# One more PSUM bank for attention while a chunk's down groups are queued, and two output tiles loaded ahead of output weights

## The chip, the cores and the metric

The kernel runs on one core of a Trainium2 chip. The core has five engines that run side by side, each with its own queue of instructions in program order: TensorE (PE in the profile; its weight loads are PEld) multiplies matrices, VectorE (DVE) and ScalarE (ACT) work element by element and are the two that empty PSUM, GpSimd (POOL) works on SBUF alone, and SyncE (SP) issues the transfers between memory and SBUF. They wait for each other through semaphores. PSUM has eight banks, each 128 partitions by 512 float32 numbers; a matmul writes into one of them, and the bank can be given to the next tile only after its last reader is done. The metric is the device time of the whole kernel in microseconds (us).

## What is computed

The reference, cut to what matters (S = 2048 tokens, D = 576, H = 32 heads of 18, F = 4608, four segments of L = 512 tokens):

```
g = sigmoid((x * gate_w).sum(-1))
# a: attention inside each segment, plus a memory of the segments before
for s in range(4):
    p = softmax(q_s @ k_s.T * scale + mask)          # causal in the segment
    o_s = sig(beta) * (phi(q_s) @ M) / (phi(q_s) @ z) + (1 - sig(beta)) * (p @ v_s)
    M += phi(k_s).T @ v_s ;  z += phi(k_s).sum()
a = concat(o_s) @ wo
# b: a gated feed-forward
b = (silu(x @ w_gate) * (x @ w_up)) @ w_down
out = g * a + (1 - g) * b
```

Every float32 operand that matters is split into a high and a low part, so that one product is three matmuls (high by high, high by low, low by high).

## The kernel before

**Three phases.** The first makes q, k, v and the memory term and writes them to DRAM scratch. The second, four fifths of the program, does two things at once: the feed-forward, and attention inside the segments. The third transposes attention's output tiles, multiplies them with the output weights, mixes with the gate and stores.

**The feed-forward sets the pace.** The hidden dimension is cut into 36 pieces f of 128; the tokens are taken in two halves (`half`). For each (half, f), the loop at L1007, seven products (`seven`, L993; Strassen's seven in place of eight) make gate and up for two blocks of 512 tokens. One `seven` is six matmuls at L998 and one at L1001, 512 columns each. They use PSUM banks 0, 1 and 2. ScalarE and VectorE combine them (L1058 to L1083), and the product of silu(gate) and up is split into `hh` and `hl` (ScalarE's copy, then VectorE's difference: L128 and L129, L940 and L941).

Three f make a chunk (`CH`, q = f % 3 is the place in it). When a chunk is complete, sixteen **down groups** are queued in `groups` (`feed`, L959): eight token tiles by two column halves. One group (`down_group`, L841) is nine matmuls (L851) into a bank, and then VectorE adds the bank into `ya` (L856; a plain copy, L854, in the first chunk).

**Ticks.** After each of the seven products, and once more between the sixth and the seventh, `tick` (L1034) is called: eight ticks k = 0 to 7 per f. A tick first issues the transfers of the down weights and then calls `beat` (L943). A beat first runs whatever was put off to it: `defer(n, fn)` puts fn n beats later, and functions of one beat run in the order in which they were put there. Then it interleaves down groups and attention. In the f after a chunk (q = 0), `SHARE` (L48) lets no group run in ticks 0 and 1, two in each of ticks 2 and 3, and three in each of the others; so the sixteen groups wait through ticks 0 and 1 and run from tick 2 on. Attention advances by one step at each such beat, by two in the beats with three groups; in f without groups it advances only in some of the ticks 0 to 4.

**Attention** is a generator (`att_gen`, L792). It works on pairs of heads; a pair of one segment is a unit of five score banks and one value product, so six steps. A step does, in this order: turn exponentials of earlier steps into float16 (`p_bank`, VectorE L752 and GpSimd L753); exponentials of the score bank of the step before (`e_bank`, ScalarE L738, which is the bank's last reader); matmuls of a new score bank (`s_bank`, TensorE L720) and its row minimum (VectorE L726). At every sixth step, in place of a score bank, the value product of the unit before (`v_unit`, TensorE L768 and L769, emptied by VectorE at L775). So a score bank taken at one step becomes free only after ScalarE's exponentials of the next step.

**Who gets which bank.** The bank of a tile is chosen while the program is written, by name, and is fixed from then on. `ts_tile` (L119) serves scores and value products: the least recently taken of banks 5, 6, 7, 3 and 4 when no group is queued, and of 5 and 6 alone as soon as `groups` holds anything, thus also in ticks 0 and 1. `group_tile` (L122) serves down groups: the least recently taken of 3, 4 and 7. `oldest` (L114) picks and notes the order.

**Where the second phase ends.** When attention has no step left, `c_open` (L864) runs once, in the beat of (second half, f = 34, tick 1). It gives attention's SBUF space to the third phase and defers, in beats: six loads of output weights (`wo_load`, L883, transfer L888, high part L891, low part L892) at beats 1, 2, 4, 5, 8 and 9; the first output tile at beat 2; the gate at 3 and 4; the second output tile at beat 6. `c_load` (L894) issues two transfers for a tile, attention's output (`o`, L897) and the memory term (`me`, L901). `c_tr` (L911) adds them on GpSimd (L913, L914), transposes on TensorE (L917, L919) and splits. A weight load needs one of four buffers named `raw`, which the last feed-forward weights still hold. SyncE issues in program order, so a transfer that waits for its buffer holds up those behind it. After the loop the third phase goes through sixteen tiles; with the first of them run the last sixteen down groups.

Of the kernel before, what the change touches and what calls it, by code (L numbers as in the profile page):

```python
# [12 lines left out]
F32 = mybir.dt.float32  # L13
# [28 lines left out]
HALF = ((2, 3), (0, 1))  # L42
TICK = ((0.57, 1.0), (0.47, 1.0))
QUIET = (5, 6, 7)
LEAD = 3
HIGH = (2, 3, 3, 7, 7, 8, 9)
LOW = (5, 6, 7, 8, 9, 10, 11)
# [18 lines left out]
def gated_mix(ctx, tc, xT, xrest, wf, wfr, wfh, wd, wv, wo, beta, cmask, ident, bmask, out):  # L66
# [3 lines left out]
    def pool(st, name, bufs, side="left", space=None):  # L70
        if space is None:
            return st.enter_context(tc.tile_pool(name=name, bufs=bufs, side=side))
        return st.enter_context(tc.tile_pool(name=name, bufs=bufs, space=space))
# [12 lines left out]
    ps = pool(ctx, "ps", 1, space=bass.MemoryType.PSUM)  # L86
# [12 lines left out]
    def banks(*ids):  # L99
        turn = cycle(ids)  # L100
        return lambda shape=(P, L): ps.tile(list(shape), F32, name=f"bank{next(turn)}")
# [8 lines left out]
    x_tile = banks(1)  # L110
    y_tile = banks(2)
    taken = {}

    def oldest(*ids):  # L114
        n = min(ids, key=lambda i: taken.get(i, 0))
        taken[n] = len(taken) + max(taken.values(), default=0) + 1
        return n

    def ts_tile(shape=(P, L)):  # L119
        return ps.tile(list(shape), F32, name=f"bank{oldest(5, 6) if groups else oldest(5, 6, 7, 3, 4)}")  # L120

    def group_tile(shape=(P, L)):  # L122
        return ps.tile(list(shape), F32, name=f"bank{oldest(3, 4, 7)}")

    groups = []

# [121 lines left out]
    def w_make(half, f, LOW=LOW):  # L248
# [5 lines left out]
        def total(j, p, q, sub=True):  # L254
            src[j] = rp.tile([P, 2, P], F32, name="ws", bufs=3)
            (nc.gpsimd.tensor_sub if sub else nc.gpsimd.tensor_add)(src[j], p(), q())  # L256
# [8 lines left out]
        def keep(j):  # L265
            nc.sync.dma_start(wc[f, j], f32(ops[j]).rearrange("p a k n -> p (a k n)"))

        todo = [(LEAD - 2, lambda: total(1, lambda: a21, lambda: a22, False)),
                (LEAD - 1, lambda: total(2, lambda: src[1], lambda: a11)),
                (LEAD + 2, lambda: total(4, lambda: a11, lambda: a21)),  # L270
                (LEAD + 4, lambda: total(5, lambda: a12, lambda: src[2]))]
        for j in range(7):
            todo += [(HIGH[j], lambda j=j: high(j)), (LOW[j], lambda j=j: low(j))]
            if half == 0 and f < KEPT:
                todo.append((LEAD + j + 3, lambda j=j: keep(j)))
        return sorted(todo, key=lambda t: t[0])
# [407 lines left out]
    with ExitStack() as st:  # L684
# [3 lines left out]
        def defer(k, fn):  # L688
            while len(due) < k:
                due.append([])  # L690
            due[k - 1].append(fn)
# [21 lines left out]
        def s_bank(z):  # L713
            u, n = divmod(z, 5)
            qs, ks = qst[u % NST], kst[u % NST]
            m = mbs[u % 2]
            t = ts_tile()
            for c, pr, i in SPLAN[n]:
                w = P * (i + 1)
                nc.tensor.matmul(t[:, c:c + w], qs[:KR, pr, P * i:P * i + P], ks[:KR, pr, 0:w],  # L720
                                 start=True, stop=True)
            for c, pr, i in SPLAN[n]:
                w = P * (i + 1)
                k = pr * 4 + i
                scr = kp.tile([P, L], BF, name="scr", bufs=1)
                nc.vector.tensor_tensor_reduce(scr[:, :w], t[:, c:c + w], cm[:, L - w:L], -SCALE, 3.0e38,  # L726
                                               OP.add, OP.min, m[:, k:k + 1])
            cur["t", z] = t
# [30 lines left out]
        def v_unit(u):  # L759
            g, hf = divmod(u, 2)  # L760
            s, b = divmod(u, 16)
            t = ts_tile([P, 2, 4, 3 * E])
            todo = [(5 * u + n, pr, i, j, c // P + j) for n in range(5) for c, pr, i in SPLAN[n] for j in range(i + 1)]
            for n, (z, pr, i, j, c) in enumerate(todo):
                h = 2 * b + pr
                v = VP[4 * s + h // 8][:, j, h % 8].rearrange("p t e -> p (t e)")
                pt = cur["x", z]
                nc.tensor.matmul(t[:, pr, i, :], pt[:, c], v, start=(n == 0), stop=False, skip_group_check=True)  # L768
                nc.tensor.matmul(t[:, pr, i, 0:2 * E], pt[:, 4 + c], v[:, 0:2 * E], start=False,  # L769
                                 stop=(n == len(todo) - 1), skip_group_check=True)  # L770
            for n in range(5):
                cur.pop(("x", 5 * u + n))
            if hf == 0:
                accs[g] = ap.tile([P, 2, 8, E], F32, name="acc")
            nc.vector.tensor_reduce(accs[g][:, hf], t.rearrange("p a i (t e) -> p (a i) e t", t=3),  # L775
                                    axis=AX.X, op=OP.add)
# [64 lines left out]
        def down_group(c, i, hf, hs, ws, ya, half):  # L841
            b, k = divmod(i, 4)
            cs = (slice(0, 320), slice(320, D))[hf]
            t = (pair_tile if cps else group_tile)([P, 320])[:, :cs.stop - cs.start]
            n = 0
            for f in range(CH * c, CH * c + CH):
                hh, hl = (z[:, b, P * k:P * k + P] for z in hs[half, f])
                d = ws[half, f]
                dh, dl = d[:, 0], d[:, 1]
                for p, q in ((hh, dh), (hh, dl), (hl, dh)):  # L850
                    nc.tensor.matmul(t, p, q[:, cs], start=(n == 0), stop=(n == 3 * CH - 1))  # L851
                    n += 1
            if c == 0:
                nc.vector.tensor_copy(ya[:, i, cs], t)  # L854
            else:
                nc.vector.tensor_add(ya[:, i, cs], t, ya[:, i, cs])  # L856
            if c == FT // CH - 1 and hf and half == 0:
                stores.append((ffd[i], ya[:, i]))


        wos, tiles = [], {}
        order = [4 * s + k for s in HALF[0] + HALF[1] for k in range(4)]

        def c_open():  # L864
            if cps:
                return
            ast.close()
            cps.append(pool(st, "cp", 2, side="right"))
            for hf in range(2):
                wos.append(cps[0].tile([P, 2, NT, 288], F32R, name=f"wo{hf}", bufs=1))  # L870
            for n, (hf, z) in zip((1, 2, 4, 5, 8, 9), ((0, 0), (0, 1), (0, 2), (1, 0), (1, 1), (1, 2))):
                wo_load(n, hf, slice(96 * z, 96 * z + 96))
            defer(2, lambda: tiles.update({0: c_load(0)}))
            defer(3, lambda: nc.scalar.activation(gg, gg, AF.Exp, scale=-1.0))
            defer(4, gates)
            defer(6, lambda: tiles.update({1: c_load(1)}))

        def gates():
            nc.vector.tensor_scalar_add(gg, gg, 1.0)
# [3 lines left out]
        def wo_load(n, hf, c):  # L883
            box = []

            def load():
                box.append(raw_tile()[:, :96 * NT].rearrange("p (k n) -> p k n", n=96))
                nc.sync.dma_start(box[0], wo[:, :, 288 * hf + c.start:288 * hf + c.stop])  # L888

            defer(n, load)  # L890
            defer(n + 5, lambda: nc.scalar.activation(wos[hf][:, 0, :, c], box[0], AF.Copy))  # L891
            defer(n + 7, lambda: nc.vector.tensor_sub(wos[hf][:, 1, :, c], box[0], f32(wos[hf][:, 0, :, c])))  # L892

        def c_load(n):  # L894
            tt = order[n]
            o = cps[0].tile([P, 640], F32, name="o", bufs=3)
            nc.sync.dma_start(o[:, 0:D], atd[tt])  # L897
            me = None
            if tt >= 4:
                me = cps[0].tile([P, D], F32, name="me", bufs=3)  # L900
                nc.sync.dma_start(me, med[tt])  # L901
            return o, me
# [40 lines left out]
        def beat(k=None, half=0):  # L943
            for fn in due.popleft() if due else ():
                fn()
            busy = 1 if groups else 0
            share = 2 if k is None else SHARE[k]
            for n in range(max(share, 1)):
                if groups and n < share:
                    down_group(*groups.pop(0))  # L950
                if n % 2 or (not busy and (n or k in QUIET)):
                    continue
                credit[0] += 0.5 if k is None else TICK[half][busy]
                if credit[0] >= 1:
                    credit[0] -= 1
                    if next(att, att) is att:
                        c_open()
# [143 lines left out]
        while next(att, att) is not att:  # L1101
            pass
        c_open()
        while due:
            for fn in due.popleft():
# [90 lines left out]
```

## Time and profile before

| what | value |
|---|---|
| median of 3 runs | 1739.13 us |
| lowest, highest | 1737.43, 1739.77 us |
| the profiled execution | 1738.29 us |
| its span, first to last instruction | 1736.6 us |
| mean granted TensorE clock | 0.998 |
| VectorE, ScalarE, GpSimd busy | 1370.0, 1094.1, 935.1 us |
| transfers | 328.05 MB, mean 189 GB/s |

How to read the rows that follow. In a timeline: start in us from the first instruction, duration in us, engine, line of the program, operation, what is written from what, shape, how many alike in a row; in square brackets the idle time of the engine before it and the operation that ended it. In a list of waits: who waited for whom, total us, times, longest. Matmuls run in a pipeline: the end of one is modelled, and the next may start before it. A group's name as L851 is a line of the kernel printed above.

### The profile page before, as it was taken

How to read it: one execution, taken by the hardware profiler on the slowest of the kernel's cores; microseconds unless marked ns; L12 is line 12 of the kernel's file. 1: busy time of each engine (PE TensorE's matmuls, PEld its weight loads, DVE VectorE, ACT ScalarE, POOL GpSimd, SP SyncE). 2: the span in 40 equal slices, each digit the busy share in tenths (PEclk: the TensorE clock that was granted, in tenths of full speed). 3: DMA queues.
4: the chain of work that ended last, by engine and by line, in shares of the span. 5: the costliest groups of instructions: out<-in, count | busy, mean ns of one | idle time of the engine just before them, and what ended most of it. 6: DMA issues, size and time to landing. Idle time of an engine off the chain costs nothing.

```text
span 1736.6 us, 34910 instructions
## 1 busy us (share of the span) xinstructions
PE 1714.6 (99%) x11868; PEld 1482.5 (85%) x11868; DVE 1370.0 (79%) x3231; ACT 1094.1 (63%) x2198; POOL 935.1 (54%) x1194
## 2 busy tenths in 40 slices
PE   9999999999999999999999999999999999999999
PEld 7899978888888888887887788888888888888899
DVE  6557588988899889887989677787888777887655
ACT  7766585776677567666755755665766576566511
POOL 4434645666666656565666455555555555555121
PEclk9999999999999999999999999999999999999999
DMA  8654499999998889997879976776778677766544
GB/s 281 237 185 155 149 306 191 222 215 203 202 232 197 176 205 207 190 190 193 205 149 266 265 173 142 180 178 162 152 180 182 139 155 180 169 135 166 157 148 137
DMA packets 524002, 328.05 MB, mean 189 GB/s; under 512 B 411184, under 2 KB 460336, under 8 KB 523824
## 3 DMA queue, kind: packets, MB, share of 16 engines
q1 hardware_dynamic: 523824, 325.83, 76.6%
q8 instruction: 93, 1.52, 0.4%
q14 instruction: 85, 0.70, 0.1%
HBM read 165.76 MB, written 76.09 MB: 139 GB/s over the span
## 4 chain that ended last, share of the span: by engine, by line
PE 81%; ACT 9%; DVE 4%; DMA 2%; issue 2%; POOL 1%; SPq 1%; DVEq 0%; ACTq 0%; POOLq 0%
PE bank L998 30%; PE bank L851 26%; PE bank L151 10%; PE bank L1001 5%; PE bank L720 4%; PE bank L768 2%; ACT L1075 1%; PE bank L769 1%; ACT L991 1%; ACT pe L738 1%; PE bank L406 1%; PE bank L452 1%; ACT row L1075 1%; PE bank L342 1%; DVE hl L941 1%
## 5 line engine op out<-in xcount | busy, mean ns | idle before, releaser
L753 POOL TENSOR_TENSOR p<-pe,p 128x512 f16<-128x512 f32 x320 | 374.9, 1171 | 454.1 <-DVE p L752 437.4
L851 PE MATMUL bank<-dw,hh 128*128 128x320 f32 (+1 forms) x2304 | 489.9, 305 | 2.7 <-ACT hh L128 1.4
L851 PEld LDWEIGHTS bank<-dw,hh 128*128 128x128 f32 x2304 | 382.6, 190 | 14.0 <-DVE ya L856 1.6
L738 ACT ACTIVATE pe<-bank,mb 128x512 f32<-128x512 f32 (+3 forms) x512 | 246.4, 523 | 218.8 <-DVE mb L726 213.4
L851 PE MATMUL bank<-dw,hl 128*128 128x320 f32 (+1 forms) x1152 | 341.1, 296 | 0.2 <-DVE hl L129 0.2
L726 DVE CUSTOM_DVE_ANT_0 scr<-bank,cm 128x512 bf16<-128x512 f32 (+3 forms) x512 | 246.3, 481 | 7.9 <-PE bank L720 1.2
L851 PEld LDWEIGHTS bank<-dw,hl 128*128 128x128 f32 x1152 | 218.6, 190 | 0.4 <-DVE hl L129 0.4
L856 DVE TENSOR_TENSOR ya<-bank,ya 128x320 f32<-128x320 f32 x352 | 157.7, 453 | 72.3 <-PE bank L851 71.6
L1001 PE MATMUL bank<-xr,rh 128*128 128x512 f32 x504 | 196.5, 390 | 0.0
L746 POOL TENSOR_SCALAR_AFFINE_SELECT pe<-pe 128x256 f32<-128x256 f32 (+1 forms) x320 | 151.1, 473 | 31.3 <-ACT pe L738 20.2
L752 DVE CAST p<-pe 128x512 f16<-128x512 f32 x320 | 147.5, 461 | 0.0
L256 POOL TENSOR_TENSOR ws<-raw 128x256 f32<-128x256 f32 x140 | 123.6, 883 | 18.3 <-DMA raw<-in_wf_dram 7.2
L720 PE MATMUL bank<-kst,qst 108*128 108x512 bf16 (+3 forms) x512 | 125.4, 306 | 4.7 <-ACT pe L738 4.7
L1001 PEld LDWEIGHTS bank<-xr,rh 128*128 128x128 f32 x504 | 94.7, 188 | 20.5
L941 DVE TENSOR_TENSOR hl<-row,hh 128x512 fp32r<-128x512 f32 x120 | 101.6, 847 | 10.9 <-ACT hh L940 10.6
L1068 ACT ACTIVATE row<-bank 128x512 f32<-128x512 f32 x72 | 43.1, 599 | 94.6 <-PE bank L1001 94.5
L1075 ACT ACT_TABLE_LOAD x72 | 92.4, 1283 | 1.3
L1073 DVE TENSOR_TENSOR row<-bank,row 128x512 f32<-128x512 f32 x72 | 49.7, 690 | 55.0 <-ACT bank L1072 54.9
L991 ACT ACT_TABLE_LOAD x72 | 92.4, 1283 | 1.0
L151 PE MATMUL bank<-xo,qhi 128*128 128x512 f32 x264 | 83.1, 396 | 0.1
L1072 ACT ACTIVATE bank<-bank 128x512 f32<-128x512 f32 x72 | 42.0, 584 | 65.0 <-PE bank L1001 64.6
L256 POOL TENSOR_TENSOR ws<-raw,ws 128x256 f32<-128x256 f32 x70 | 56.6, 808 | 48.4 <-DVE wo__22573 L263 10.9
(2166 smaller groups left out, 4119.1 us busy)
## 6 DMA issues: line engine op xcount, KB each, us to landing
raw<-in_wf_dram SPq DMA_DIRECT2D x140, 256.0 KB
rh<-rc SPq DMA_DIRECT2D x72, 336.0 KB
dc<-dw SPq DMA_DIRECT2D x36, 576.0 KB
dw<-dc SPq DMA_DIRECT2D x36, 576.0 KB
stk<-q SPq DMA_DIRECT2D x32, 384.0 KB
draw<-in_wd_dram SPq DMA_DIRECT2D x36, 288.0 KB
rc<-rt SPq DMA_DIRECT2D x42, 224.0 KB
vd<-vps SPq DMA_DIRECT2D x8, 912.0 KB
```

The lines of the kernel that those rows point to most:

```text
L151: nc.tensor.matmul(t, st[n], mv[n], start=(n == 0), stop=(n == 13))
L256: (nc.gpsimd.tensor_sub if sub else nc.gpsimd.tensor_add)(src[j], p(), q())
L720: nc.tensor.matmul(t[:, c:c + w], qs[:KR, pr, P * i:P * i + P], ks[:KR, pr, 0:w], start=True, stop=True)
L726: nc.vector.tensor_tensor_reduce(scr[:, :w], t[:, c:c + w], cm[:, L - w:L], -SCALE, 3.0e38, OP.add, OP.min, m[:, k:k + 1])
L738: nc.scalar.activation(pe[:, c:c + w], t[:, c:c + w], AF.Exp, bias=m[:, k:k + 1], scale=SCALE)
L746: nc.gpsimd.affine_select(d, d, pattern=pat, compare_op=OP.is_ge, fill=0.0, base=0, channel_multiplier=1)
L752: nc.vector.tensor_copy(p[:, 0], pe)
L753: nc.gpsimd.tensor_sub(p[:, 1], pe, p[:, 0])
L851: nc.tensor.matmul(t, p, q[:, cs], start=(n == 0), stop=(n == 3 * CH - 1))
L856: nc.vector.tensor_add(ya[:, i, cs], t, ya[:, i, cs])
L998: nc.tensor.matmul(t, w[:, p, z], x[z][:, q], start=first and n == 0, stop=False, skip_group_check=True)
L1001: nc.tensor.matmul(t, rem[:, RPOS[j]], XR[j], start=False, stop=True, skip_group_check=True)
```

## The change

Two things are changed. First, the choice of banks. While all sixteen groups of a chunk are still queued (so in ticks 0 and 1 of the f after a chunk), scores and value products choose among banks 5, 6 and 7 in place of 5 and 6. The order of taking is replaced by a clock that goes up by one at each bank taken by attention or a group and at each beat; a bank that attention takes is noted as taken `HELD` = 4 units later than the clock, a group's bank 1 unit later, and the lowest note is picked. Second, in `c_open`, the loads of the first two output tiles are deferred ahead of the output weights: the first stays at beat 2 but comes before the weight load of that beat, the second moves from beat 6 to beat 3.

```diff
+HELD = 4
...
     taken = {}
-
-    def oldest(*ids):
+    clock = [0]
+
+    def soonest(ids, held):
         n = min(ids, key=lambda i: taken.get(i, 0))
-        taken[n] = len(taken) + max(taken.values(), default=0) + 1
+        clock[0] += 1
+        taken[n] = clock[0] + held
         return n
 
     def ts_tile(shape=(P, L)):
-        return ps.tile(list(shape), F32, name=f"bank{oldest(5, 6) if groups else oldest(5, 6, 7, 3, 4)}")
+        ids = (5, 6, 7, 3, 4) if not groups else (5, 6, 7) if len(groups) == 16 else (5, 6)
+        return ps.tile(list(shape), F32, name=f"bank{soonest(ids, HELD)}")
 
     def group_tile(shape=(P, L)):
-        return ps.tile(list(shape), F32, name=f"bank{oldest(3, 4, 7)}")
+        return ps.tile(list(shape), F32, name=f"bank{soonest((3, 4, 7), 1)}")
...
                 wos.append(cps[0].tile([P, 2, NT, 288], F32R, name=f"wo{hf}", bufs=1))
+            defer(2, lambda: tiles.update({0: c_load(0)}))
+            defer(3, lambda: tiles.update({1: c_load(1)}))
             for n, (hf, z) in zip((1, 2, 4, 5, 8, 9), ((0, 0), (0, 1), (0, 2), (1, 0), (1, 1), (1, 2))):
                 wo_load(n, hf, slice(96 * z, 96 * z + 96))
-            defer(2, lambda: tiles.update({0: c_load(0)}))
             defer(3, lambda: nc.scalar.activation(gg, gg, AF.Exp, scale=-1.0))
             defer(4, gates)
-            defer(6, lambda: tiles.update({1: c_load(1)}))
...
             for fn in due.popleft() if due else ():
                 fn()
             busy = 1 if groups else 0
+            clock[0] += 1
```

## The prediction

> **What bounds the kernel.** I read the page first, then TensorE's own waits, then the timeline around each wait.
>
> ```profile
> span 1736.6 us, 34910 instructions
> PE 1714.6 (99%) x11868; PEld 1482.5 (85%) x11868; DVE 1370.0 (79%) x3231; ACT 1094.1 (63%) x2198; POOL 935.1 (54%) x1194
> ```
>
> TensorE (PE) is busy for 1714.6 of 1736.6 us; no other engine comes near. Whatever the change wins must come out of the 22 us in which it stands idle, or out of gaps that the busy time hides. The next view says for whom it stood: line, who released it, total us, times, longest.
>
> ```profile
> PE bank L720 <- ACT pe L738: 4.7, 6, 1.2
> PE bank L768 <- ACT pe L738: 3.1, 2, 1.9
> ...
> PE bank L917 <- POOL o L913: 1.1, 1, 1.1
> ```
>
> L720 is a score matmul, L768 the first matmul of a value product, and L738 the exponentials that empty a score bank. So eight times, 7.8 us in all, attention found no free bank. L917 is the transpose of an output tile and waited once for L913, which adds its two loaded halves. These three rows are what the change can reach. One stall in full, on TensorE:
>
> ```profile
> 624.85 0.39 PE L1001 MATMUL bank<-xr,rh 128*128 128x512 f32 x1
> 626.39 0.38 PE L720 MATMUL bank<-kst,qst 108*128 108x512 bf16 x1 [1.16 <-ACT pe L738]
> ...
> 628.01 0.39 PE L1001 MATMUL bank<-xr,rh 128*128 128x512 f32 x1
> 628.24 0.46 PE L851 MATMUL bank<-dw,hh 128*128 128x320 f32 x2
> ...
> 632.49 0.30 PE L851 MATMUL bank<-dw,hh 128*128 128x320 f32 x1
> ```
>
> Without a wait the next matmul starts 0.23 us after L1001 (628.24 - 628.01). Here it starts 1.54 us after: 1.31 us is lost, 0.16 more than the 1.16 that is printed as idle. Counting L1001 matmuls puts this stall at tick 1 of f = 21: the sixteen down groups of a chunk have been queued, none has run, and the score tile may take bank 5 or 6 only. All eight stalls lie at tick 1 of such an f (two were value products, in the same place). L851 at 628.24 is the chunk's first down group.
>
> [...]
>
> **The change, part by part.** *Third bank.* I wrote out which bank each tile takes under both rules. The order of instructions on every engine stays what it was (outside the two output tiles), and so do all durations; only the waits on banks move. In each of the 22 chunks whose groups start at tick 2, one of the two score or value tiles of ticks 0 and 1 now takes bank 7. In all eight stalled places the tile then finds a bank that was emptied over 4 us earlier, going by the times of before. Removed: 7.8 + 8 x 0.16 = **9.1 us**. Two more score matmuls lose under 0.3 us together; I count them at nothing.
>
> *What comes in its place.* Bank 7 is then missing for the first groups. Before, the third group (tick 3) took a bank that attention had left long ago. Now, in the 14 chunks where bank 7 went out at tick 1, the first groups have banks 3 and 4 alone, so the third takes the first one's bank and must wait for VectorE's add (L856, L854 in the first chunk) of the first group. The rows: the add, then the third group's first matmul.
>
> ```profile
> 390.00 0.30 PE L851 MATMUL bank<-dw,hh 128*128 128x320 f32 x1
> 390.28 0.48 DVE L856 TENSOR_TENSOR ya<-bank,ya 128x320 f32<-128x320 f32 x1
> ...
> 1477.83 0.48 DVE L856 TENSOR_TENSOR ya<-bank,ya 128x320 f32<-128x320 f32 x1
> 1478.14 0.30 PE L851 MATMUL bank<-dw,hh 128*128 128x320 f32 x1
> ```
>
> At 390 the add ends at 390.76 (0.76 after the matmul started); with 0.05 us for the signal, the lag at which the eight stalls ended, TensorE would wait 0.81 us. At 1478 it ends at 1478.31: 0.21. In the other twelve the add ends 0.15 to 1.7 us before the matmul of before, so nothing is due there unless TensorE comes earlier, and in the stalled chunks it does. Is VectorE able to come earlier too? In the chunk of the stall above:
>
> ```profile
> 625.65 0.69 DVE L129 TENSOR_TENSOR hl<-row,hh 128x512 fp32r<-128x512 f32 x1 [1.22 <-ACT hh L128]
> ...
> 630.68 1.22 DVE L941 TENSOR_TENSOR hl<-row,hh 128x512 fp32r<-128x512 f32 x1
> 631.82 0.48 DVE L856 TENSOR_TENSOR ya<-bank,ya 128x320 f32<-128x320 f32 x1
> ```
>
> These are the first and the last two of eleven rows; only the first prints an idle time. From 625.65, where ScalarE releases it, to the add's end at 632.30 VectorE runs without a gap; it is behind, not waiting for TensorE. So the add stays where it is. The third group started at 632.49; 1.31 us earlier is 631.18, and it would wait until 632.35: 1.17 of the 1.31 us is given back. The same subtraction, first and last stalled chunk (the stall, the add, the third group):
>
> ```profile
> 262.80 0.22 PE L720 MATMUL bank<-kst,qst 108*128 108x128 bf16 x1 [0.93 <-ACT pe L738]
> 267.52 0.48 DVE L854 COPY ya<-bank 128x320 f32<-128x320 f32 x1
> 268.87 0.30 PE L851 MATMUL bank<-dw,hh 128*128 128x320 f32 x1
> ...
> 1591.80 0.19 PE L768 MATMUL bank<-v,pt 128*128 128x57 bf16 x1 [1.22 <-ACT pe L738]
> 1596.90 0.48 DVE L856 TENSOR_TENSOR ya<-bank,ya 128x320 f32<-128x320 f32 x1
> 1598.54 0.30 PE L851 MATMUL bank<-dw,hh 128*128 128x320 f32 x1
> ```
>
> First: won 0.93 + 0.16 = 1.09, add over at 268.00, so 268.05 - (268.87 - 1.09) = 0.27 back. Last: won 1.38, add over at 1597.38, 0.27 back. The six between these two, by the same working: 1.17 (above), 0.33 in one, 0.2 in one (up to 0.4; there VectorE has a gap and can follow in part), nothing in three. Returned in the eight: 2.2. New waits in all: 0.81 + 0.21 + 2.2 = **3.3 us**; from below 1.0, if every add follows TensorE; from above 9.1 + 1.0, if the eight give everything back.
>
> *Held longer.* A score bank counts as taken 4 units later than a group's 1. At a chunk's end the first free score tile so prefers a group's bank. By the times of before, the closest such pick leaves 0.9 us and the others more: nothing.
>
> *Two output tiles.* Tile 0's loads go ahead of the second output-weight load, tile 1's ahead of the third. SyncE's queue runs in order:
>
> ```profile
> 1622.69 6.78 SPq L888 DMA_DIRECT2D raw<-in_wo_dram  x2
> ...
> 1635.98 1.46 SPq L888 DMA_DIRECT2D raw<-in_wo_dram  x2
> 1637.49 0.62 SPq L897 DMA_DIRECT2D o<-atd  x1
> ...
> 1645.78 0.66 PE L917 MATMUL bank<-idt,o 128*128 128x128 f32 x4 [1.09 <-POOL o L913]
> ...
> 1649.21 0.65 DVE L892 TENSOR_TENSOR wo<-raw,wo 128x480 fp32r<-128x480 f32 x1
> ...
> 1650.00 0.32 PE L151 MATMUL bank<-wo,oh 128*128 128x288 f32 x1
> ```
>
> The weight loads (L888) wait for buffers, and tile 1 (1637.49) stood behind the pair at 1635.98. In the new order it goes out at about 1630, 7 us earlier, and L917's wait of 1.09 + 0.16 = 1.25 us goes. No weight load is held up, since those wait for buffers longer than two issues take. What is late next: the last low part of the output weights (L892) ends at 1649.86, and the matmul that reads it starts at 1650.00. Only 0.14 us is won unless that weight arrives earlier, which two tile loads out of its way may give by 0.2 us. I take **0.4 us**; between nothing and 1.25.
>
> **The sum.** 9.1 - 3.3 + 0.4 = 6.2 us. The profiled execution took 1738.29 us (span 1736.6 and 1.7 around it): 1732.1. The median of the three runs is 0.84 us above it, which would make 1732.9. I start between the two, at 1738.7, and say **1732.5 us**, 0.4% faster. Runs of before spread over 2.3 us, so about 0.2%, 3.5 us, is what a measurement tells from no change.
>
> **Rivals.** (a) *VectorE follows*: the adds move up with TensorE, only 1.0 us of new waits is left, 9.1 - 1.0 + 0.4 = 8.5: about 1730.2. Against it is the unbroken VectorE stretch. 0.12. (b) *The wait returns elsewhere*: what frees the bank is itself late (ScalarE and VectorE behind), so TensorE, come early, stops at the third group or at the next half tile, and all but some 2 us goes back: 1736.7, or nothing at all won, 1738.7. For it: the five chunks above that give some back; against it: in the stalled chunks the other bank takes leave over 1.5 us, more than all but one of the stalls. 0.17. [...] The stalls here are single waits for a bank, which speaks for a gain. (c) *Slower*: the third group's wait for the first one's add grows in all 14 chunks. Its price: were each add one VectorE operation of 1.22 us (L941 above) later against TensorE, the 14 waits (lag, plus what TensorE is early, less what the add had to spare) would add up to about 18.4 us, so 18.4 - 9.1 - 0.4 = 8.9 slower: 1747.6. It decides from about 13 us, 0.9 a chunk; only the chunk at 390 shows such a size, and VectorE's list is unchanged. 0.07. (d) *Without effect*: the third bank isn't the one that frees the stalled tile; 1738.7. 0.04. The forecast keeps 0.60.
>
> **Range and chances.** The forecast's own range, from its bounds and the spread of runs, is 1729.5 to 1735.5. With most of (a) and half of (b): 1728.7 to 1737.0. Faster by over 0.2% (below 1735.6): the forecast, (a) and the edge of (b), 0.74; within 0.2%: the rest of (b), (d) and part of the forecast's edge, 0.19; slower: (c), 0.07.
>
> **What would show it.** Right: TensorE's waits for L738 at L720 and L768 fall from 7.8 us to under 1; new waits at L851 for L856 of 2 to 4 us appear, the longest near 390 and in the chunk of f = 21; L917's wait for L913 is gone. Wrong: waits for L738 stay (then (d)); L851's waits exceed 6 us ((b) or (c)); or they stay near 1 us ((a)).

## The result, and the profile after

| kernel | median us | lowest to highest | runs | ratio to before, 95% interval |
|---|---|---|---|---|
| before, beside after | 1738.38 | 1735.97 to 1739.77 | 17 | |
| after | 1734.68 | 1733.1 to 1737.38 | 17 | 0.9981 [0.9975, 0.9988] |

The change is worth 3.3 us by the ratio (0.0019 x 1738), 3.7 by the medians. The forecast was 6.2 us and 1732.5; the time lies in its range, and the gain is little more than half of what the sum said. So the question is which terms of the sum are missing.

Line numbers of the changed kernel lie 4 above those of before between L128 and L947 (L851 is L855, L856 is L860, L738 is L742, L892 is L896, L913 is L917) and 5 above behind that (L998 is L1003). The page of after, and TensorE's waits in it (line, who released it, total us, times, longest):

```profile
span 1732.8 us, 34911 instructions
...
PE 1713.9 (99%) x11868; PEld 1479.9 (85%) x11868; DVE 1371.7 (79%) x3231; ACT 1094.0 (63%) x2198; POOL 935.4 (54%) x1194
```

```profile
PE bank L855 <- DVE ya L860: 4.1, 4, 2.0
...
PE bank L155 <- DVE wo L896: 1.1, 1, 1.1
PE bank L1003 <- DVE row L1087: 0.8, 1, 0.8
PE bank L855 <- ACT pe L742: 0.6, 1, 0.6
```

The two rows of before with 7.8 us (scores and value products waiting for exponentials) and the row of L917 are gone. Of the rows above, three are new; the wait for an add was there before too, once, with 1.3 us at the end of the first half, and is now 4.1 us in four. Three of the four are the forecast ones (the timeline shows two of them: add, then the third group), the fourth and longest, 2.0 us, lies at the end of the first half:

```profile
388.37 0.48 DVE L860 TENSOR_TENSOR ya<-bank,ya 128x320 f32<-128x320 f32 x1
...
388.90 0.56 PE L855 MATMUL bank<-dw,hh 128*128 128x320 f32 x2 [0.65 <-DVE ya L860]
...
630.55 0.48 DVE L860 TENSOR_TENSOR ya<-bank,ya 128x320 f32<-128x320 f32 x1
...
631.08 0.56 PE L855 MATMUL bank<-dw,hh 128*128 128x320 f32 x2 [0.96 <-DVE ya L860]
```

```profile
930.02 0.56 PE L855 MATMUL bank<-dw,hh 128*128 128x320 f32 x2 [0.59 <-ACT pe L742]
...
931.45 0.39 PE L724 MATMUL bank<-kst,qst 108*128 108x512 bf16 x1
933.85 0.51 PE L855 MATMUL bank<-dw,hh 128*128 128x256 f32 x2 [2.01 <-DVE ya L860]
```

The last three rows are TensorE at the end of the first half, where the sixteen groups of the last chunk run one after the other with no gate and up products between them. I had left this chunk out of the sum. In before TensorE waited 1.34 us for an add at the same place (937.71).

**Where the time went.** TensorE runs the same 11868 matmuls in the same order in both traces, so the n-th of one can be set against the n-th of the other. The difference of their starts (after less before) is a curve that steps wherever one kernel stalls and the other doesn't. Its steps, added up by place (places in the time of before):

| place | steps, us | sum |
|---|---|---|
| the eight stalls (263, 626, 808, 1114, 1174, 1352, 1413, 1592 us) | -1.07 -1.31 -2.03 -0.74 -0.49 -0.88 -1.07 -1.37 | -9.0 |
| the third down group (269, 390, 632, 817, 1419, 1478, 1599) | +0.37 +0.91 +1.22 +0.77 +0.41 +0.32 +0.36 | +4.4 |
| behind the stall at 808, at half clock in before | | -1.4 |
| end of the first half, 830 to 967 | -3.86 becomes -1.88 | +2.0 |
| third phase, from 1600 on | +0.60 -1.13 -0.18 +0.39 +0.43 +1.37 and small ones | +1.5 |
| the first 60 us, which the change doesn't touch | | -0.7 |
| small steps elsewhere (292, 307, 448, 830) | -0.24 -0.40 -0.21 +0.20 | -0.6 |
| all | | -3.8 |

A third group's step is the wait for the add (0.80 near 390, 1.11 at 632; 3.7 in all) and mostly 0.11 more at the matmul behind it: after a wait the second matmul starts 0.25 us after the first, without one 0.14.

The +2.0 is not the two waits of 930 to 934 (0.59 and 2.01 us). Up to 938 of before's time the curve is where it was at 900 (-3.86): before stood and ran slowly there too. What was lost is 1.5 us to a stretch of half clock behind these waits in after, and 0.5 at 967, where TensorE waits 0.84 us for VectorE's L1087. In the second profile of the same kernel (below) the two waits are the same, no half clock follows (the mean granted clock is 1.0), and 1.7 us are lost at 963 to 967 in waits for ScalarE and for weights.

The first two rows of the table are the core of the prediction. The next three are what it lacked: the clock and the end of the first half were not in the sum, and the third phase has the other sign.

**The third phase in rows.** After, VectorE, GpSimd and TensorE around the wait for L896, the last low part of the output weights:

```profile
1643.90 1.63 POOL L917 TENSOR_TENSOR o<-o,me 128x576 f32<-128x576 f32 x1 [12.23 <-DMA me<-med]
...
1644.19 1.87 DVE L896 TENSOR_TENSOR wo<-raw,wo 128x480 fp32r<-128x480 f32 x1
...
1646.11 0.53 PE L155 MATMUL bank<-wo,oh 128*128 128x288 f32 x2 [1.11 <-DVE wo L896]
```

In before the last of these subtractions took 0.65 us (the row at 1649.21 in the prediction). Here it takes 1.87 us, and it runs from 1644.19 to 1646.06 while GpSimd adds the halves of the third output tile. TensorE waits 1.11 us for it. The same thing at an earlier place, VectorE's L1083 (L1088 after) and GpSimd's add of the first output tile; before, then after:

```profile
1633.32 0.68 DVE L1083 TENSOR_TENSOR row<-row 128x512 f32<-128x512 f32 x1
```

```profile
1627.66 1.43 POOL L917 TENSOR_TENSOR o<-o,me 128x576 f32<-128x576 f32 x1
...
1628.04 1.60 DVE L1088 TENSOR_TENSOR row<-row 128x512 f32<-128x512 f32 x1
```

The same operation on the same shape: 0.68 us alone, 1.60 beside GpSimd. In before GpSimd's add started at 1634.21, after this operation had ended (1634.00); the tiles that come earlier have put the two side by side.

Which subtraction is hit varies between profiles. In the second profile of after the last low part takes 0.69 us, and the subtraction that makes `hl` (L133) lies beside the add instead; TensorE waits for that:

```profile
1644.28 1.74 POOL L917 TENSOR_TENSOR o<-o,me 128x576 f32<-128x576 f32 x1 [11.53 <-DMA me<-med]
...
1645.10 1.47 DVE L133 TENSOR_TENSOR hl<-row,hh 128x512 fp32r<-128x512 f32 x1 [0.35 <-ACT hh L132]
...
1646.62 0.41 PE L855 MATMUL bank<-dw,hl 128*128 128x320 f32 x1 [0.94 <-DVE hl L133]
```

The same pair, 1.46 us for the split of `hl` and 0.69 for the last low part, stands in four more kernels with early tiles below: the tiles alone, `HELD` = 1, the six banks, and bank 7 in the first beat; TensorE's longest wait for `hl` is 0.9 us in each. So it is the stretching that repeats, not the operation that it hits.

### The profile page after: what moved, and what is told of

It is laid out like the page before. It is cut to its first block, busy times and chain, and to the rows that moved or that the text cites. A ratio compares the mean times of both kernels' runs of the same rounds, so it can differ in the third digit from the quotient of the medians.

```text
span 1732.8 us, 34911 instructions
## 1 busy us (share of the span) xinstructions
PE 1713.9 (99%) x11868; PEld 1479.9 (85%) x11868; DVE 1371.7 (79%) x3231; ACT 1094.0 (63%) x2198; POOL 935.4 (54%) x1194
## 4 chain that ended last, share of the span: by engine, by line
PE 81%; ACT 7%; DVE 5%; issue 3%; DMA 3%; POOL 2%; SPq 0%; DVEq 0%; POOLq 0%; ACTq 0%
PE bank L1003 31%; PE bank L855 25%; PE bank L155 10%; PE bank L1006 5%; PE bank L724 4%; PE bank L772 2%; PE bank L773 1%; ACT L1080 1%; PE bank L410 1%; ACT L996 1%; DMA stk<-q 1%; DVE scr L730 1%; DVE hl L945 1%; PE bank L456 1%; PE bank L346 1%
## 5 line engine op out<-in xcount | busy, mean ns | idle before, releaser
L855 PE MATMUL bank<-dw,hh 128*128 128x320 f32 (+1 forms) x2304 | 491.2, 306 | 6.7 <-DVE ya L860 4.1
L855 PEld LDWEIGHTS bank<-dw,hh 128*128 128x128 f32 x2304 | 381.5, 190 | 21.0 <-DVE ya L860 7.7
L742 ACT ACTIVATE pe<-bank,mb 128x512 f32<-128x512 f32 (+3 forms) x512 | 246.1, 522 | 219.9 <-DVE mb L730 214.5
L855 PE MATMUL bank<-dw,hl 128*128 128x320 f32 (+1 forms) x1152 | 341.1, 296 | 0.3 <-DVE hl L133 0.3
L855 PEld LDWEIGHTS bank<-dw,hl 128*128 128x128 f32 x1152 | 218.6, 190 | 0.9 <-DVE hl L133 0.9
L860 DVE TENSOR_TENSOR ya<-bank,ya 128x320 f32<-128x320 f32 x352 | 158.1, 453 | 72.1 <-PE bank L855 71.2
L1077 ACT ACTIVATE bank<-bank 128x512 f32<-128x512 f32 x72 | 42.0, 584 | 67.0 <-PE bank L1006 66.7
L1063 ACT ACTIVATE bank<-bank 128x512 f32<-128x512 f32 x72 | 41.7, 579 | 65.4 <-PE bank L1006 65.3
```

The source lines that it names most:

```text
L742: nc.scalar.activation(pe[:, c:c + w], t[:, c:c + w], AF.Exp, bias=m[:, k:k + 1], scale=SCALE)
```

## The experiments

My theory after the result: (1) the third bank is worth what the stalls were, 9.0 us; (2) the order of holding (`HELD` = 4), which I had put at nothing, makes the third down group go back to the first one's bank; (3) the early tiles cost time, since GpSimd's adds then run beside VectorE's subtractions and stretch them; (4) too few banks cost the rest at the end of the first half. Rivals: the tiles' transfers and not the adds hold up the weights; the waits of groups and attention are interchangeable, so that whoever gets the bank, somebody waits.

Each ratio below is to before, run beside it on the same chip. Before took 1738.45 us beside the two halves of the change, `HELD` = 1 with the early tiles, and the earlier low part; 1740.05 beside the holding order alone, the kernel without adds, the six banks and bank 7 in the first beat with the early tiles; 1739.62 beside the four of the last table.

**The two halves of the change alone.** The third bank and the holding order, with the tiles where before loads them:

```diff
-            defer(2, lambda: tiles.update({0: c_load(0)}))
-            defer(3, lambda: tiles.update({1: c_load(1)}))
             for n, (hf, z) in zip(...
+            defer(2, lambda: tiles.update({0: c_load(0)}))
...
             defer(4, gates)
+            defer(6, lambda: tiles.update({1: c_load(1)}))
```

> The new choice of banks alone (third bank and HELD = 4); the two output tiles are loaded where they were before. First theory: the whole gain is the third bank's. In the profiles the changed kernel is 5.4 us ahead of the one before when the third phase begins and 3.8 ahead at the end, so this kernel should be about 5 us faster than before, and no slower than the whole change. Rival: the tile loads carry a good part of the gain; then this kernel is 2 to 3 us faster than before only.

Measured: 1734.56 us (1732.86 to 1736.51, 8 runs), 0.9974 [0.9964, 0.9985]. Its waits:

```profile
PE bank L855 <- DVE ya L860: 4.0, 4, 2.0
...
PE bank L921 <- POOL o L917: 1.0, 1, 1.0
```

The groups' waits are those of after and the wait for the output tile is back; the curve of starts stands at -4.83 us at the end of the second half and at -4.73 at the end of the program. So with the old loads the third phase loses next to nothing. By the ratio the gain is 4.5 us, near the 5 that were expected.

And the tiles alone, with the banks of before (so the numbering is that of before):

> The two output tiles loaded early, banks as before. First theory: TensorE no longer waits for the second tile (1.1 us), but meets the last low part of the output weights instead, so the time stays within 1 us of before, on either side (0 to 1.5 us slower if VectorE's last split again runs beside GpSimd's add). Rival: the tile loads are worth what the wait was, 1.0 to 1.25 us faster.

Measured: 1740.83 us (1739.35 to 1741.94, 11 runs), 1.0012 [1.0003, 1.0021]: slower. TensorE's waits:

```profile
PE bank L720 <- ACT pe L738: 4.7, 7, 1.0
PE bank L768 <- ACT pe L738: 3.1, 2, 1.9
...
PE bank L998 <- ACT bank L1072: 1.3, 2, 1.1
...
PE bank L851 <- DVE hl L129: 1.1, 2, 0.9
```

All 7.8 us of the old stalls stand, L917's wait is gone, and two others of 1.1 and 0.9 us, both for work of ScalarE and VectorE in the third phase, have come in its place. By the curve, 1.9 us are lost in that phase, and 2.1 by the ratio, a little more than the 1.5 that were allowed for. The move is a loss by itself, not a small gain that the banks hide.

**The order of holding.** As after, with one number changed:

```diff
-HELD = 4
+HELD = 1
```

> The changed kernel with HELD = 1 in place of 4, so attention's banks are noted like the groups'. First theory: holding bank 7 back is what makes the third group wait for the first one's add on VectorE (0.65, 0.96, 0.51 and 0.13 us in the profile). With HELD = 1 the third group takes bank 7, whose exponentials leave some 0.5 us by the times of before; those waits go, and the kernel is 2 to 3 us faster than the changed one, about 1732. Rival: the holding protects the groups from exponentials that are late; then waits of groups for the exponentials appear and the kernel is 2 us or more slower than the changed one.

Measured: 1734.15 us (1733.43 to 1735.24, 7 runs), 0.9971 [0.9961, 0.9982].

```profile
PE bank L772 <- ACT pe L742: 1.8, 2, 1.0
...
PE bank L724 <- ACT pe L742: 1.5, 2, 1.0
...
PE bank L855 <- DVE ya L860: 0.3, 1, 0.3
```

The waits for adds fell from 4.1 to 0.3 us: the third groups' went, as expected; the one at the end of the first half is shorter here beside a half clock of 6.83 us (mean granted clock 0.998), and is 1.7 with the old loads (below). But waits for exponentials came back at later ticks (mostly at 642, 646 and 827 us): 3.3 us. By the ratios the kernel is 1.7 us better than after, with intervals that overlap; 2 to 3 were expected. The notes of the code say why the first part holds. Take the chunk at 390: a score takes bank 7 at tick 1 when the clock shows c + 1 and is noted c + 5. At tick 2 the first group takes bank 3 and is noted c + 4, the second takes bank 4 and is noted c + 6. The third picks the lowest of c + 4, c + 6 and c + 5: bank 3, that of the first group, whose add has just begun. With `HELD` = 1 bank 7 is noted c + 2 and the third group gets it.

The holding order without the third bank (tiles as in before):

```diff
-        ids = (5, 6, 7, 3, 4) if not groups else (5, 6, 7) if len(groups) == 16 else (5, 6)
+        ids = (5, 6, 7, 3, 4) if not groups else (5, 6)
```

> The holding order alone (HELD = 4 and the new clock), without the third bank and with the old order of the tiles. The prediction put "held longer" at nothing: by it the time is that of before, 1738.4 us, within 0.4, with the same eight waits of L724 and L772 for the exponentials of L742 (7.8 us). The rival: with two banks for attention while groups stand, the added holding sends scores to banks that the groups have just used and the other way round; a replay of the bank turns on the times of before leaves two of the old waits and makes new ones of 4.2 us near 927, 1.9 us near 870 and five of 0.8 to 1.0 us, some 10 us in place of 7.8: 1739 to 1744 us.

Measured: 1739.46 us (1737.73 to 1742.6, 11 runs), 1.0002 [0.9993, 1.0011]: no difference.

```profile
PE bank L772 <- ACT pe L742: 7.8, 5, 4.1
PE bank L724 <- ACT pe L742: 5.2, 6, 1.0
```

The waits grew, as the replay said, and by more: 13.0 us in place of 7.8 (some 10 expected), with 4.1 us near 927. But the time didn't follow. The curve peaks at +7.4 us near 937, stands at 3.0 by 971 and at -0.5 at the end; between 971 and the end it falls because the five old stalls there are gone, against two new ones. Of the drop before 971 I take it that a wait of TensorE just ahead of the groups of the last chunk lets VectorE and the transfers catch up, and is paid back there; no run separates that. Sums of waits don't add up to time around that place.

**GpSimd's adds.** As after, but the memory term is not added in the first four output tiles:

```diff
+            added[0] += 1
-            if me is not None:
+            if me is not None and added[0] > 4:
                 nc.gpsimd.tensor_add(o[:, 0:D], o[:, 0:D], me)
```

> As after, but GpSimd's add of the memory term (L917) is left out for the first four output tiles, so those 512 rows of the output lack it; loads and all else stay. Theory: the third phase lost its gain because these adds run beside VectorE's operations with two SBUF inputs (L1088 1.60 us for 0.68, the last low part of the output weights L896 1.87 us for 0.65). Then L896 near 1644 takes 0.65 us, TensorE's wait L155 for L896 (1.1 us) goes, and the time falls by 1.0 to 2.0 us against after, to 1732.7 to 1733.7. Rival: the DMA transfers started in another order set the late weight, and the adds only happen to lie there: L896 stays as late, the wait stays, and the time is within 0.4 us of after's 1734.7.

Measured: 1734.4 us (1732.45 to 1735.83, 7 runs), 0.997 [0.9959, 0.998], so about 1.9 us better than after by the ratios (0.9981 - 0.997). In the third phase L1091 (L1088 of after) and L896:

```profile
1642.33 0.68 DVE L1091 TENSOR_TENSOR row<-row 128x512 f32<-128x512 f32 x1
...
1643.64 0.66 DVE L896 TENSOR_TENSOR wo<-raw,wo 128x480 fp32r<-128x480 f32 x1 [0.63 <-ACT wo L895]
...
1645.27 0.65 DVE L896 TENSOR_TENSOR wo<-raw,wo 128x480 fp32r<-128x480 f32 x1
```

Loads and their order are those of after; the last low part takes 0.65 us in place of 1.87, TensorE's wait for it is gone, and the curve gains 0.9 us in this phase where after loses 1.5. The rival, late transfers, falls. The 0.9 is not the worth of the early transfers alone: without the adds the transposes don't wait for them either. (The two ratios' intervals overlap; the verdict rests on the rows.)

A way round the collision, the last low part one beat earlier:

```diff
-            defer(n + 7, lambda: nc.vector.tensor_sub(wos[hf][:, 1, :, c], ...
+            defer(n + (6 if n == 9 else 7), lambda: nc.vector.tensor_sub(wos[hf][:, 1, :, c], ...
```

> The changed kernel with the low part of the last output weight split one beat earlier, so ahead of the last feed-forward split on VectorE. First theory: in the third phase TensorE waits 1.11 us for that low part because it runs 1.87 us, in place of 0.65, beside GpSimd's add of the third output tile; moved ahead of that add it runs in 0.65, the wait goes, and about 1 us is won over the changed kernel. Rival: the low part is late because its weight lands late; then the move wins at most 0.2 us.

Measured: 1735.79 us (1732.31 to 1740.07, 11 runs), 0.9985 [0.9976, 0.9994]. No gain; a miss.

```profile
1647.00 1.60 POOL L917 TENSOR_TENSOR o<-o,me 128x576 f32<-128x576 f32 x1 [11.83 <-DMA me<-med]
...
1649.03 0.72 DVE L133 TENSOR_TENSOR hl<-row,hh 128x512 fp32r<-128x512 f32 x1
...
1649.81 0.41 PE L855 MATMUL bank<-dw,hl 128*128 128x320 f32 x1 [1.54 <-DVE hl L133]
```

The subtraction still met GpSimd's add (1.87 us), now ahead of L133 in VectorE's queue; the low part `hl` came late instead, and TensorE waited 1.54 us for that. (The profile is of the slowest of the eleven runs, 1740.07 us, and has 3.41 us at half clock behind this wait.)

**The end of the first half.** As after, with the three banks of the gate and up products open to down groups in the ten beats there:

```diff
-        return ps.tile(list(shape), F32, name=f"bank{soonest((3, 4, 7), 1)}")
+        ids = (3, 4, 7, 0, 1, 2) if wide[0] and len(groups) > 6 else (3, 4, 7)
+        return ps.tile(list(shape), F32, name=f"bank{soonest(ids, 1)}")
...
+                    wide[0] = True
                     for n in range(BREAK):
                         beat(None if n > 1 else n)
+                    wide[0] = False
```

This kernel changes the computation (I take it to be the second half's first gate and up products, which accumulate in banks that groups have written); the operations and their sizes stay. (Its lines from L128 on are 2 above those of after.)

> As after, but in the ten beats after the first half, when the three banks of the gate rows are idle, down groups may use them as well (six banks until six groups are left). Theory: the two waits of L855 there, 0.59 us for an exponential that sits in bank 7 and 2.01 us for the adds of L860, come from too few banks, and the 3.41 us at half clock that follows costs 1.5 us: without them the time falls by 2.5 to 4 us against after, to 1730.7 to 1732.2. Rival: VectorE is behind there whatever the banks, and the wait comes back in the next chunk's first beat for a bank that its adds still hold: 1734 to 1735.

Measured: 1736.9 us (1734.97 to 1738.17, 11 runs), 0.9983 [0.9974, 0.9992]: no better than after. Waits and windows of that stretch (window; its length; busy us and count of PE, PEld, DVE, ACT and POOL; granted clock; share of the DMA engines; GB/s):

```profile
PE bank L857 <- DVE ya L862: 4.0, 5, 1.4
...
PE bank L1005 <- DMA wo__13416<-wc: 1.4, 1, 1.4
...
PE bank L1005 <- DMA wo__13458<-wc: 0.7, 1, 0.7
```

```profile
935.00:945.00 10.00, 9.17 (x69) 8.73 (x68) 10.00 (x20) 3.17 (x5) 8.56 (x8) 1.00 1.09 290
945.00:956.00 11.00, 9.70 (x57) 8.12 (x58) 10.08 (x23) 5.14 (x11) 5.94 (x6) 1.00 1.13 254
```

The curve goes from -1.8 at 900 to -5.0 at 938, so the groups do run earlier, by 3.2 us; by 967 it is at 0.02. VectorE is busy for all 10 us of one window and the DMA engines are fully taken in both (shares of 1.09 and 1.13), and the products that follow wait for weights (`wo_` from `wc`) still on their way. The rival was right in the outcome: banks are not what bounds this stretch. What came back were a wait of 1.40 us for an add (at 945.57) and waits for weights; that VectorE and the transfers set the bound is read from these windows.

**Bank 7 in the first beat only.** The third bank without the groups' wait, by giving bank 7 away at tick 0 alone and keeping it free in the f before (`where` holds the tick and q):

```diff
-        ids = (5, 6, 7, 3, 4) if not groups else (5, 6, 7) if len(groups) == 16 else (5, 6)
+        ids = ((5, 6, 3, 4) if where[1] == CH - 1 else (5, 6, 7, 3, 4)) if not groups else (7,) if len(groups) == 16 and where[0] == 0 else (5, 6)
```

> As after (tiles loaded early too), but while a chunk's first beat runs, attention's one score takes bank 7 and nothing else does, and the beat before a chunk leaves bank 7 alone; later beats have two banks as in before. Theory: the third down group then finds bank 7 drained in all chunks, so the waits of L855 for the add L860 (4.0 us in 4 rows, and some 1.5 us in small ones) go and the waits of L724 and L772 for exponentials do not come back: 2 to 4 us less than after, 1731 to 1733. Rival: as with HELD = 1, where the group's wait went and waits of 3.3 us for exponentials came back at later beats: 1733.7 to 1735.

Measured: 1734.41 us (1732.63 to 1737.22, 9 runs), 0.9972 [0.9962, 0.9982]. (L856 and L861 here are L855 and L860 of after.)

```profile
PE bank L856 <- DVE ya L861: 2.0, 1, 2.0
...
PE bank L725 <- ACT pe L743: 1.5, 2, 1.0
...
PE bank L773 <- ACT pe L743: 1.1, 2, 0.9
```

Of the groups' waits for adds only the one at the end of the first half is left; 2.6 us for exponentials came back, as with `HELD` = 1. So the rival was right, and the 2 to 4 us that were expected over after are 1.6 by the ratios, with intervals that overlap. At the end of the second half it stands 6.5 us ahead of before, and loses 1.9 of them in the third phase, like after.

**Together, with the old loads.** After itself again, and three kernels with the tiles loaded where before loads them.

> The changed kernel itself once more, to stand beside the other kernels on this chip. Both theories expect what it had before: 0.998 of before's time, some 3.5 us less, its waits of L855 for the adds L860 at 4 us in all and the last low part L896 (near 1644) at 1.87 us beside GpSimd's add.

> The third bank with HELD = 1 and the output tiles where before loads them. Theory: as with HELD = 1 alone the groups' waits go and waits for exponentials of some 3.3 us stand in their place, and without the moved tiles 1 to 2 us come back in the third phase: 1.5 to 2.5 us less than after in the same call, 0.9965 to 0.9975 of before, and 0.5 to 1 us more than the kernel that gives bank 7 away only in the first beat. Rival: the order of holding doesn't matter and the tiles don't either: within 0.7 us of after.

> Bank 7 goes to attention in a chunk's first beat alone (and stays free in the beat before), and the output tiles are loaded where before loads them. Theory: the two losses of after are separate, so leaving both out adds up: without the moved tiles about 1 to 2 us, without the groups' waits about 1.2 us (the trace with the tiles moved stood 6.5 us ahead of before at the end of the second half, after 5.4): 2 to 3 us less than after in the same call, 0.996 to 0.997 of before. Rival: what is won in the chunks comes back as waits for weights that are still on their way (wo_ from wc) at the start of the second half, since their transfers leave by beats: within 0.7 us of after.

> The kernel that gives bank 7 to attention in a chunk's first beat alone, with HELD = 1 in place of 4 and the tiles where before loads them. Theory: with bank 7 out of the way HELD decides nothing, as a replay of the bank turns finds a bank free in time by either order: within 0.7 us of the same kernel with HELD = 4. Rival: HELD = 4 keeps scores off banks that the last groups have just used, so without it waits of L724 and L772 of some 0.4 to 1 us come back: 1 to 3 us slower than with HELD = 4.

| kernel | median us | runs | ratio to before, 95% interval | curve at 1592, at the end |
|---|---|---|---|---|
| after again | 1736.05 | 9 | 0.9982 [0.9972, 0.9991] | -4.6, -2.3 |
| third bank, `HELD` = 1, old loads | 1729.66 | 5 | 0.9949 [0.9937, 0.9962] | -8.6, -8.7 |
| bank 7 at tick 0 only, old loads | 1732.69 | 5 | 0.9962 [0.995, 0.9975] | -3.1, -3.1 |
| the same with `HELD` = 1 | 1732.19 | 5 | 0.9956 [0.9943, 0.997] | -8.3, -8.6 |

In after again the time and the waits for adds (4.6 us) are as expected, but the last low part takes 0.69 us and not 1.87, as shown above. The waits of the second of these kernels:

```profile
PE bank L855 <- DVE ya L860: 1.7, 1, 1.7
...
PE bank L724 <- ACT pe L742: 1.4, 2, 1.0
...
PE bank L772 <- ACT pe L742: 1.1, 2, 0.8
```

With `HELD` = 1 and the tiles left alone the kernel is about 8.9 us faster than before and 5.7 us faster than after (0.9949 against 0.9982; the intervals don't meet): a version that beats both. It won more than expected. By the curve against the kernel with the third bank, `HELD` = 4 and old loads, it gains 4.2 us at seven third groups, gives 2.9 back in waits for exponentials (at 290, 642, 646, 706 and 827), and wins 2.3 between 963 and 966, where its weights land in time. That last part is not shown to be the order's work: the kernel with `HELD` = 1 and early tiles is the same program up to there and lost 1.7 at this place. So the order itself is worth 1.3 us by the curve. The five runs of the kernel lie at 1729.3 to 1729.7 (three, the profiled one among them), 1732.9 and 1734.1. None of the three kernels with old loads loses in the third phase, and after loses 1.9 again (behind the third group at 1599). With bank 7 given away at tick 0 alone, `HELD` makes no difference (the intervals lie over one another), as the replay said. The three medians can't be ranked by these runs: their intervals overlap, and profiles of like kernels differ by up to 2 us at 963 to 967 and by a few tenths in the first 60 us. The column of the curve is of one run for each kernel: with bank 7 at tick 0 it is the slowest of five for `HELD` = 4 (1735.22) and the fastest of five for `HELD` = 1 (1729.77).

## Why the prediction was right, and where it was not

- **Removed: 9.1 us.** Right: 9.0 by the curve, all eight stalls gone, and the half-speed stretch of 1.4 us behind the longest of them too, which I hadn't counted.
- **New waits of the third group: 3.3 us.** Right in place and nearly in size: 3.7 of waits, the longest at f = 21 (1.11 for 1.17) and near 390 (0.80 for 0.81). VectorE was behind, as its unbroken stretch showed. One was mis-sized: 0.66 in the chunk at 817. The matmul behind each wait costs 0.11 more, which I counted for the stalls and not here: 4.4 in all.
- **"Held longer: nothing".** This step failed. I looked for a late bank at a chunk's end, and there, in the kernel that holds longer with two banks, waits of 4.1 us appeared that the end of the first half absorbed. What counted was the groups' side: the price of the third group's wait, which I booked under the third bank, comes from `HELD` = 4. With `HELD` = 1 the third group takes bank 7 and these waits go; with the old loads that is worth 4.2 us by the curve, less 2.9 given back to waits for exponentials.
- **Two output tiles: 0.4 us won.** Wrong in sign: 1.5 us lost in the profile of after, 1.9 in the second one, and slower by itself (1.0012). The 1.13 us of L917 came as forecast. I had named the last low part L892 as the next limit and looked only at whether its transfer would come earlier; I did not look at which engine would then run beside it. GpSimd's add moved next to it and made 0.65 us into 1.87, or, in the second profile, next to the split of `hl` and made 0.68 into 1.47. Leaving four adds out brought the phase to a gain of 0.9.
- **Left out: the chunk at the end of the first half.** +2.0 us: 1.5 to half clock and 0.5 to a later wait in this profile, 1.7 to waits at 963 to 967 in the second. The waits of 0.59 and 2.01 us for banks cost nothing against before. Six banks didn't help. Why TensorE stands at 963 to 967 in some profiles and not in others whose program is the same up to there stays open.
- **Sum.** 9.0 - 4.4 - 2.0 - 1.5, and 1.4 + 0.7 + 0.6 from the clock, the first 60 us and small steps, make 3.8 us in the profiles. That the median came within 2.2 us of the forecast is in part luck: the half-speed stretch that I left out paid part of the losses that I left out.
- **Rivals.** (a) didn't happen: VectorE did not follow. (b) happened in small: part of the gain went back at the third groups and at the end of the first half. (c) needed 0.9 us in each of 14 chunks; one wait was longer (1.11) and one near it (0.80). (d) is excluded by the eight stalls.

## What to carry to other kernels

When an operation is moved earlier, list what each engine will then run beside it, not only what waits in its queue: here a subtraction on VectorE took 1.87 us beside an add on GpSimd, and 0.65 without one. When a rule chooses a shared bank by age, write its notes out for both sides that take banks; a bonus meant for one side changes the pick of the other. And set two traces of the same order against each other matmul by matmul: the steps show gains and losses by place that a single total hides.

## What the runs showed of the hardware

**VectorE beside GpSimd.** In these traces operations of VectorE with two float32 inputs in SBUF took longer beside GpSimd's: L896, L1088 and L133 above, and L263 (128x256) over the whole of before, with 416 ns on average in the 173 cases with no GpSimd operation beside it and 813 ns in the 284 that lay for over 60% of their time beside one. L856 (128x320), with one input in PSUM, did not change: 488 and 484 ns. As to how long: L896 of after began 0.29 us into GpSimd's add and ended at 1646.06, 0.53 us after that add was over at 1645.53, where its normal time is 0.65. Why this is so was not shown.

**Half clock for 3.41 us.** TensorE's granted clock fell to half for 3.41 us at a time, twice in before (from 809.0 and 931.9) and once in after (from 934.4), after stalls shorter than that. TensorE's stall in before, and windows of before and of after (columns as above; the clock is the third number from the end):

```profile
808.15 0.19 PE L768 MATMUL bank<-v,pt 128*128 128x57 bf16 x1 [1.88 <-ACT pe L738]
```

```profile
809.50:812.50 3.00, 3.00 (x8) 2.33 (x9) 1.55 (x3) 0.95 (x3) 3.00 (x5) 0.51 0.56 98
931.00:934.00 3.00, 2.76 (x12) 2.50 (x13) 2.91 (x8) 2.28 (x7) 1.84 (x3) 0.65 1.01 359
```

```profile
930.00:934.00 4.00, 1.97 (x11) 1.57 (x12) 3.78 (x5) 1.52 (x3) 4.00 (x5) 1.00 1.13 272
934.00:937.50 3.50, 3.50 (x17) 3.50 (x18) 3.50 (x8) 1.32 (x2) 3.42 (x3) 0.56 1.11 334
```

In before it followed the stall of 1.88 us at 808 and cost 1.4 us by the curve; in after it followed the waits of 0.59 and 2.01 us at 930 to 934 and cost 1.5 against the second profile of after, which has none there. The other one of before, from 931.9 on, behind a wait of 1.35 us for ScalarE, cost next to nothing: TensorE was slower, and then waited less for the add. The stalls are not the only condition: the kernel with the tiles alone has the same stall (1.9 us in its waits), and its mean granted clock of 0.999 leaves room for one such stretch and not for two, as in before (0.998); and the same waits of 0.59 and 2.01 us had none behind them in the second profile of after, with the banks alone, and with bank 7 in the first beat and early tiles (mean granted clock 1.0 in each). The clock fell behind 1.88 us of idle in one place, and behind 0.59 and 2.01 us in another. What exactly decides it stays open.
